# Reordering the prologue of a chunked recurrence: the first triangular inverse ahead of the last two preparations

## The chip, the cores and the metric

The kernel runs on one core of a Trainium2 chip. The metric is the device time of one execution in microseconds. The core has five engines that matter here, each with an instruction queue worked in order: TensorE (PE), VectorE (DVE), ScalarE (ACT), GpSimd (POOL), and SyncE (SP), which issues the DMA transfers. Instructions of different engines are ordered by semaphores alone.

## The reference, cut to what matters

A matrix-valued recurrence is followed by a small mixture of four attention experts. The recurrence has 4 batches of 8 heads, 768 steps and head size 40:

```python
for t in range(S):
    y[:, :, t] = einsum('bhd,bhde->bhe', r_t, state)
    Sa = einsum('bhde,bhe->bhd', state, a_t)
    state = state * w_t[:, :, None, :] - einsum('bhd,bhe->bhde', Sa, b_t)
    state = state + einsum('bhd,bhe->bhde', v_t, k_t)
```

Its output, with the heads side by side, is `x` (4 x 768 x 320). Each expert computes causal softmax attention over `x`; two of the four experts count for each token, weighted by a gate. The change touches the recurrence alone.

## The kernel before, in words

**Chunks, windows, units.** The 768 steps are cut into 24 chunks of 32 steps. Four chunks make a window (6 windows). The 32 (batch, head) pairs make 4 groups of 8. A unit is one chunk of one group: 96 units, unit u being chunk u // 4, group u % 4. A window therefore holds 16 units.

**Preparations.** For each window and group there is a preparation (`prep(i)`, i = 4 x window + group, 24 in all). Its pieces have one-letter names, and the schedule strings are made of them: `a` suffix scan of the decays (DVE, L249, into the tile SUF), `c` reciprocal (DVE), `s` prefix scan (DVE, L255), `x` scaled a (DVE, L259 or L263, into AB), `k`, `l` scaled k and b (DVE, L268, into KB) or `p`, both at once on POOL (L265), `b` a small copy (ACT), `d`, `q` copies of AB into the tile GL (ACT for i < 8, POOL L274 after), `m`, `n` products of KB and AB on TensorE (L284 or L286) whose results DVE masks into GL (L288, two multiplications each), `o` two DMAs of a part of GL to DRAM (L293, tensor Ld), `w`, `e`, `v` DMA loads of the inputs of preparation i + 1.

**Inverses.** Each window needs the inverse of unit triangular 32x32 matrices. `L` fetches them from Ld into the tile MT (L304, SP), `C` sets the diagonal (POOL memset, L306), `T5` issues five of the row instructions (L320), `A`, `D`, `E` (or `A`, `B`) transpose column ranges of MT into TT (DVE, L322). The first inverse does half of the rows on DVE (28 instructions) and the rest with products on TensorE (`P`, `F`, `H`). Inverses 1 to 5 run all 60 row instructions on POOL, where each depends on the one before. Window W needs inverse W from its first unit on (step `u` reads TT), and inverse W needs the four preparations of window W.

**The order.** All engines follow one order of issue. `START` is the prologue, read from left to right. Then the loop counts n from 0 to 99. For each n it issues seven steps, each of another unit, in the order of `MAIN`: `u` of unit n - 1, `g` of unit n, `y` of n - 3, `f` of n - 2, `t`, `k`, `v`. After each step it issues the jobs that were put into that slot with `at(n, slot, ...)`: slots 0 to 6 are the slash-separated fields of the strings in `EARLY`, `SIDE`, `SIDE2` and `INV`, so that `///6mno` stands in slot 3, behind the step `f`. `SIDE`, `SIDE2` and `INV` are relative to n0 = 16 (W - 1). Step `f` ends with a mask multiplication on DVE (L409), for which the step `y` of the next n waits.

**Loads.** Inputs of the preparations go to three tiles, EW, EA and EK. The first eight preparations borrow space of other tiles (`E8`) so that their loads need not wait; `own` are the tiles of all the later ones. A load into `own` waits for the preparation that read it before.

Of the kernel before, what the change touches and what calls it, by code (L numbers as in the profile page):

```python
# [17 lines left out]
NW, NG, C = 6, 4, 32  # L18
NKB = 10

START = """Z0 E4 0acsxklb E5 E7 E6 1acsxkl W2 0d 0q 1b 2ap 0mno 2csx W4 1d 1q 2b 3ap 1mno 3csx W0 2d 2q 4ap W1 3b 2mno 3mno L W3 V00 V10 3d 3q
4csx W5 W6 5ap C 4b 4mno V01 V11 5csx Z1 4d 4q Y0 6ap 5b 5mno k0 g0 6csx 5d 5q Y1 7ap E8 6b 6mno 7csx T14 7mno 7b 6d 6q Y2 T14 A B P F0 8ac H0 7d 7q Y3 8s 8w 8x 8v"""
EARLY = {
    1: "////F1",
    2: "////H1",
    4: "////F2",
    5: "////H2",
    7: "////F3",
    8: "////H3",
# [19 lines left out]
}  # L49

SIDE2 = {
    -16: "///0bkl///0e",
    -15: "///1ac",
    -14: "///1s///1w",
    -13: "///1x///1v",
    -12: "///1bkl///1e",
    -11: "///2ac 0m",
    -10: "///2s 1m///2w",
    -9: "///2bx///2v",
    -8: "///2kl///2e",  # L60
    -7: "///3ac 2m",
    -6: "///3s///3w",
    -5: "///3bx///3v",
    -4: "///3kl 0no//0dq/3e",
    -3: "///3m 1no//1dq",
    -2: "///2no//2dq",
    -1: "///3no//3dq",
}
INV = {0: "L C T5", 1: "T5", 2: "T5", 3: "T5", 4: "T5", 5: "T5", 6: "T5", 7: "T5", 8: "T5", 9: "T5", 10: "T5///A", 11: "T5", 14: "///D", 16: "E"}


def layouts(r, k, v, w, a, b):
# [47 lines left out]
def recurrence(tc, ctx, I, xT, CM, early, tail=None):  # L120
# [5 lines left out]
    V, A, T, PL = nc.vector, nc.scalar, nc.tensor, nc.gpsimd  # L126

    def ps(shape):
        return pp.tile(shape, F32, name="ps", tag="ps", bufs=4)
# [4 lines left out]
    def ring(name, shape, n):  # L134
        return [sp.tile(shape, F32, name=f"{name}{i}") for i in range(n)]
# [7 lines left out]
    D1P = ring("D1P", [104, 528], 1)[0]  # L143
    SUF = ring("SUF", [104, 529], 1)[0]
    PC2 = ring("PC", [104, 2, 4], 6)
    SC2 = ring("SC", [104, 2, 16, 33], 6)
    PC, SC = ([t[k // 2][:, k % 2] for k in range(12)] for t in (PC2, SC2))
    KB = ring("KB", [128, 16, 64], NKB)
# [9 lines left out]
    LS = ring("LS", [128, 32, 40], 2)  # L158
# [4 lines left out]
    XT = ring("XT", [104, 8, 128], 2)  # L163
# [3 lines left out]
    flat = lambda t: t.rearrange("p a b -> p (a b)")  # L167
# [3 lines left out]
    own = (EWr[0], EAr[0], EKr[0])  # L171
    thirds = lambda t: (t[:, 0:528], t[:, 528:1040], t[:, 1040:2064])
    E8 = [own, thirds(r20), (flat(SC[11]), flat(LS[1])[:, 0:512], g1[:, 0:1024]), thirds(r21),
          (flat(SC[8]), flat(XT[1][:, 4:8]), flat(KB[8])), (flat(SC[9]), flat(XT[1][:, 0:4]), flat(KB[9])), own, (flat(SC[10]), flat(LS[1])[:, 512:1024], flat(XT[0]))]

    SUFs = SUF, flat(TT[0])[0:104, 0:529]

    def load_e(i, k):
        if i < 24:
            t = (E8[i] if i < 8 else own)[k]  # L180
            src, c0 = (("EA", 0), ("EA", 528), ("EK", 0))[k]
            nc.sync.dma_start(t[0:104], I[src][i, :, c0:c0 + t.shape[1]])
# [56 lines left out]
    def prep(i):  # L239

        w, g = divmod(i, NG)
        ab, sc, kb, pc = ABr[i % 4], SC[i % 12], KB[i % NKB], PC[i % 12]
        gl = GL[w % 2]
        SUF = SUFs[1 if i in (1, 3, 5, 7) else 0]
        sv = SUF[:, 1:529].rearrange("p (n c) -> p n c", c=33)
        EW, EA, EK = (x[0:104] for x in (E8[i] if i < 8 else own))
        ea = EA.rearrange("p (n c) -> p n c", c=32)
        def f0a():
            V.tensor_tensor_scan(SUF[:, 0:528][:, ::-1], EW[:, ::-1], d1[:, ::-1], 1.0, op0=OP.mult, op1=OP.add)  # L249
        def f0b():  # L250
            A.activation(pc, sv[:, ::4, 0], AF.Copy)
        def f0c():
            V.reciprocal(D1P[:, 0:528:132], sv[:, ::4, 0])
        def f1():
            V.tensor_tensor_scan(sc.rearrange("p n c -> p (n c)"), EW, D1P, 0.0, op0=OP.mult, op1=OP.add)  # L255
        aa = flat(ab)[0:104, 0:512].rearrange("p (n c) -> p n c", c=32)
        def f2():
            if i < 8:
                V.tensor_tensor(aa, ea, sc[:, :, 0:32], op=OP.mult)  # L259
                return  # L260
            for s in range(2):
                q = slice(64 * s, 64 * s + 40)
                V.tensor_tensor(ab[q, :, 32 * s:32 * s + 32], ea[q], sc[q, :, 0:32], op=OP.mult)  # L263
        def fp():
            PL.tensor_tensor(kb[0:104].rearrange("p n (k c) -> p n k c", k=2), EK.rearrange("p (n k c) -> p n k c", n=16, k=2),  # L265
                             sv[:, :, None, 1:33].to_broadcast([104, 16, 2, 32]), op=OP.mult)
        def fk(k):
            V.tensor_tensor(kb[0:104, :, 32 * k:32 * k + 32], EK.rearrange("p (n k c) -> p n k c", n=16, k=2)[:, :, k], sv[:, :, 1:33], op=OP.mult)  # L268
        def f5(s):
            o, q = gl[64:104, g, :, s, :], slice(64 * s, 64 * s + 40)  # L270
            if i < 8:
                A.activation(o, aa[q], AF.Copy)
            else:
                PL.tensor_copy(o, ab[q, :, 32 * s:32 * s + 32])  # L274
        def mm(c):
            p_a = ps([128, 4, 2, 32])
            o = gl[0:64, g].rearrange("q (p c) s t -> q p c s t", p=4)
            for p in range(4):
                for x in range(2):
                    n = p * 4 + c + x  # L280
                    if i < 8:
                        for s in range(2):
                            q = slice(64 * s, 64 * s + 40)
                            T.matmul(p_a[64 * s:64 * s + 64, p, x], kb[q, n, :], aa[q, n, :], start=True, stop=True, tile_position=(64 * s, 64 * s))  # L284
                    else:
                        T.matmul(p_a[64 * x:64 * x + 64, p], kb[0:104, n, :], ab[0:104, n, :], start=True, stop=True, tile_position=(0, 64 * x))  # L286
            for x in range(2):
                V.tensor_tensor(o[:, :, c:c + 2, x] if i < 8 else o[:, :, c + x], p_a[64 * x:64 * x + 64],  # L288
                                maskn[x][:, None, None, :].to_broadcast([64, 4, 2, 32]), op=OP.mult)
        def f6():  # L290
            for s in range(2):
                b = 64 * (g // 2) + 32 * s + 16 * (g % 2)
                nc.sync.dma_start(Ld[w % 2][b:b + 16].rearrange("n j t -> j n t"), gl[32:64, g, :, s])  # L293
        def load(k):
            load_e(i + 1, k)
        return dict(a=f0a, b=f0b, c=f0c, s=f1, x=f2, p=fp, k=lambda: fk(0), l=lambda: fk(1), d=lambda: f5(0), q=lambda: f5(1),
                    m=lambda: mm(0), n=lambda: mm(2), o=f6, w=lambda: load(0), v=lambda: load(1), e=lambda: load(2))
# [156 lines left out]
    def at(n, s, *fs):  # L454
        jobs.setdefault((max(n, 0), s), []).extend(fs)

    P = [prep(i) for i in range(24)]

    def run(i, names):
# [3 lines left out]
    for W in range(1, NW):  # L463
        n0 = 16 * (W - 1)
        inv = invert(W)
        for r, line in (SIDE if W > 2 else SIDE2).items():
            if W == 1:
                break
            for k, part in enumerate(line.split("/")):
                for z in part.split():  # L470
                    at(n0 + r, k, *[P[4 * W + int(z[0])][x] for x in z[1:]])
        for r, line in INV.items():
            for k, part in enumerate(line.split("/")):
                for z in part.split():
                    at(n0 + r, k, lambda z=z, inv=inv: inv[z[0]](*[int(x) for x in [z[1:]] if x]))
# [3 lines left out]
    def seq(line):  # L479
        for z in line.split():  # L480
            if z[0] == "E":
                for k in (0, 2, 1):
                    load_e(int(z[1:]), k)
            elif z[0] == "Y":
                zero(flat(ABr[int(z[1])])[:, 0:512])
            elif z[0] == "W":
                rest(int(z[1]))
            elif z[0] == "Z":
                zgl(int(z[1]))
            elif z[0] == "V":  # L490
                for k in (0,) if z[2] == "0" else (2, 1):
                    load_c(int(z[1]), k)
            elif z[0] == "k":
                units[int(z[1])]["k"]()
            elif z[0] == "g":
                units[int(z[1])]["g"]()
            elif z[0] in inv:
                inv[z[0]](*[int(x) for x in [z[1:]] if x])
            else:
                run(int(z[0]), z[1:])  # L500
# [7 lines left out]
    units = [unit(u) for u in range(NU)]  # L508
    seq(START)
    for n, line in EARLY.items():  # L510
# [473 lines left out]
```

## Time and profile before

| | |
|---|---|
| median of 3 runs | 638.88 us (636.87 to 639.97) |
| profiled execution | 635.57 us, span 633.8 us |
| PE, DVE, ACT, POOL busy over the span | 88%, 77%, 75%, 54% |
| first step `u` of a unit (L393) | 67.88 us |
| last row instruction of the fifth inverse ends | 324.07 us |

Times within the profile count from the start of its span. The last column of the stretches read below is the rate of the DMA engines in GB/s, the one before it their busy share, and the one before that the granted TensorE clock as a share of full speed.

### The profile page before, as it was taken

Reading aid. Unit: us, or ns where it says so; the run is one execution under the profiler, and the core shown is the slowest. Engines: PE = TensorE matmul, PEld = TensorE weight load, DVE = VectorE, ACT = ScalarE, POOL = GpSimd, SP = SyncE. Lnnn points to the kernel's source line nnn. Section 1 sums busy time; section 2 is a strip of 40 time slices with the busy share of each in tenths; the row PEclk is TensorE's granted clock in tenths of the full one; section 3 lists DMA queues with packets and bytes.
Section 4 is the critical chain, followed back from the end, with each engine's and each line's share of the span. In section 5 each row is a group of like instructions: output and inputs, shape, how many; then the busy total and the mean of one; then the engine's idle time right before and its main releaser. Section 6 shows DMA issues by size and latency. Waiting matters only on the chain. (4 is left out here: it accounts for less than half of the span.)

```text
span 633.8 us, 22437 instructions
## 1 busy us (share of the span) xinstructions
PE 558.9 (88%) x8849; PEld 480.2 (76%) x8849; DVE 488.9 (77%) x1150; ACT 477.2 (75%) x1299; POOL 345.4 (54%) x491
## 2 busy tenths in 40 slices
PE   6463899998998898899998997899899999999995
PEld 6463787886887787788886777778778778887774
DVE  7978678899999989986666947688885886677661
ACT  7991579899889879988999984576666666676763
POOL 2330399569989988988830101354662545243631
PEclk9555589999999999999999999899999999999999
DMA  7882344685678477545249716222321132102001
GB/s 224 240 195 50 103 114 113 142 206 155 138 184 185 114 186 192 144 95 174 74 146 259 212 39 167 51 63 76 83 60 47 39 89 66 47 12 61 32 33 49
DMA packets 63690, 73.84 MB, mean 117 GB/s; under 512 B 30168, under 2 KB 48344, under 8 KB 63576
## 3 DMA queue, kind: packets, MB, share of 16 engines
q1 hardware_dynamic: 63432, 72.21, 43.4%
q8 instruction: 73, 1.20, 0.8%
q14 instruction: 41, 0.34, 0.2%
q10 hardware_dynamic: 144, 0.10, 0.1%
HBM read 54.99 MB, written 11.01 MB: 104 GB/s over the span
## 5 line engine op out<-in xcount | busy, mean ns | idle before, releaser
L833 POOL TENSOR_TENSOR P<-P,m 128x128 f32<-128x128 f32 (+2 forms) x96 | 87.7, 935 | 95.4 <-DVE m L829 46.3
L320 POOL TENSOR_TENSOR MT<-MT,TP 128x30 f32<-128x30 f32 (+9 forms) x150 | 97.1, 647 | 11.8
L320 POOL TENSOR_TENSOR TP<-MT 128x30 f32<-128x30 f32 (+9 forms) x150 | 95.0, 633 | 11.6
L416 PE MATMUL py<-R,LS 128*40 128x80 f32 x1536 | 86.2, 238 | 4.2 <-DVE R L409 1.6
L822 ACT ACTIVATE P<-sc,m 128x128 f32<-128x128 f32 (+2 forms) x96 | 60.8, 634 | 29.8 <-DVE m L821 23.5
L821 DVE TENSOR_REDUCE m<-sc 128x1 f32<-128x128 f32 (+2 forms) x96 | 59.4, 622 | 20.1 <-PE sc L814 18.8
L416 PEld LDWEIGHTS py<-R,LS 128*40 128x40 f32 x1536 | 64.1, 119 | 13.1 <-ACT LS L446 5.1
L409 DVE TENSOR_TENSOR R<-ps,CM 64x128 f32<-64x128 f32 x192 | 54.9, 286 | 23.4 <-PE ps L406 19.7
L811 PE MATMUL sc<-ks,qs 128*128 128x384 f32 (+4 forms) x256 | 62.5, 345 | 5.4 <-ACT P L822 5.1
L395 ACT ACTIVATE R<-ps 32x160 f32<-32x160 f32 x192 | 56.7, 295 | 4.8 <-PE ps L393 0.8
L387 ACT ACTIVATE GT<-ps 32x160 f32<-32x160 f32 x192 | 56.6, 295 | 3.4
L841 PE MATMUL pt<-CM,P 128*128 128x128 f32 x336 | 51.9, 276 | 2.1 <-ACT pt L847 1.7
L406 PE MATMUL ps<-RB,VU 128*64 128x64 f32 x768 | 46.5, 229 | 2.7 <-ACT VU L401 1.9
L811 PEld LDWEIGHTS sc<-ks,qs 128*128 128x128 f32 x256 | 40.6, 189 | 10.8 <-ACT P L822 9.6
L393 PE MATMUL ps<-GT,TT 128*33 128x80 f32 x768 | 46.8, 243 | 2.0 <-ACT GT L387 1.0
L446 ACT ACTIVATE LS<-pt 40x320 f32<-40x320 f32 x92 | 39.6, 431 | 11.7 <-PE pt L442 8.9
L377 ACT ACTIVATE LS<-pt 64x320 f32<-64x320 f32 x96 | 41.5, 433 | 8.8 <-PE pt L373 7.3
L733 PE MATMUL pt<-xh,wq 128*128 128x384 f32 x192 | 43.0, 359 | 3.5 <-POOL xh L712 1.5
L859 PE MATMUL ot<-pt,vv 128*64 128x256 f32 (+1 forms) x384 | 43.5, 359 | 0.0
L442 PE MATMUL pt<-CM,R 104*104 104x104 f32 x368 | 42.8, 260 | 0.0
L406 PEld LDWEIGHTS ps<-RB,VU 128*64 128x64 f32 x768 | 36.7, 140 | 8.0 <-ACT VU L401 6.8
L847 ACT ACTIVATE pt<-pt 128x512 f32<-128x512 f32 (+1 forms) x64 | 34.5, 543 | 10.0 <-PE pt L841 8.8
(160 smaller groups left out, 1334.1 us busy)
## 6 DMA issues: line engine op xcount, KB each, us to landing
RB<-in_RB SPq DMA_DIRECT2D x24, 320.0 KB
EK<-in_EK SPq DMA_DIRECT2D x18, 416.0 KB
ks<-ks SPq DMA_DIRECT2D x32, 192.0 KB
R<-in_VG SPq DMA_DIRECT2D x24, 208.0 KB
EW<-in_EA SPq DMA_DIRECT2D x18, 214.5 KB
R<-in_VT SPq DMA_DIRECT2D x48, 80.0 KB
R<-in_RT SPq DMA_DIRECT2D x24, 160.0 KB
xT<-XT SPq DMA_DIRECT2D x48, 80.0 KB
```

Of the source, the lines that this page charges most:

```text
L320: return [lambda: e.tensor_tensor(tmp, row, col, op=OP.mult), lambda: e.tensor_tensor(o, o, tmp, op=OP.add)]
L387: A.activation(gt[b:b + 32, s::2], p_g[64 * s:64 * s + 32], AF.Copy)
L393: T.matmul(p_u[64 * x:64 * x + 33, y], tt[:, o:o + 33], gt[:, 2 * p:2 * p + 2], start=True, stop=True, tile_position=(0, 64 * x))
L395: A.activation(hd(r2[32:64, 40 * h0:40 * h0 + 320], 80)[:, x::2], p_u[64 * x:64 * x + 32], AF.Copy, scale=-1.0)
L406: T.matmul(p_f[64 * x:64 * x + 64, y], vu[:, p, :], rb[:, 4 * g + p, :], start=True, stop=True, tile_position=(0, 64 * x))
L409: V.tensor_tensor(o[:, :, x], p_f[64 * x:64 * x + 64], mask[x][:, None, None, :].to_broadcast([64, 2, 2, 32]), op=OP.mult)
L416: T.matmul(py[64 * s:64 * s + 40, p], ls[:, h, :], m, start=True, stop=True, tile_position=(0, 64 * s))
L811: T.matmul(ps[:, c, 0:cw], QS[b][:, e, o], KS[b][:, e, z, k], start=(z == 0), stop=(z == 1 and not last), skip_group_check=True)
L821: V.tensor_reduce(m[:, 0, t:t + 1], ps[:, 0:ch, 0:cw], axis=AX.XY, op=OP.max, negate=True)
L822: later(DE, lambda: A.activation(pv, ps[:, 0:ch, 0:cw], AF.Exp, bias=m[:, 0, t:t + 1], accum_out=m[:, 1, t:t + 1]))
L833: PL.tensor_tensor(P[:, 0:n], P[:, 0:n], m[:, 3, t:t + 1].to_broadcast([128, n]), op=OP.mult)
L841: T.transpose(p[:, 128 * y:128 * y + 128], st["P"][t][:, 128 * c:128 * c + 128], ident)
```

## The change

Preparations 6 and 7 leave the prologue in good part. The rows of the first inverse (`T10`, `T18`) and its transposes (`A B P`) now stand directly behind `5csx` and `5mno`. Preparation 6 follows them: its `acsxpb` ends the prologue, its `mno` comes in loop step n = 0. Preparation 7 is spread over n = 0 to 3 and uses the `own` tiles and the first SUF tile. Its load `E7` is the last item of `START`; `E6` comes after `V10`. The second inverse (W = 1), which fetched at n = 0 and issued five rows a unit from there on, fetches at n = 4 and issues its 60 rows at once; its last transpose `E` moves from slot 0 to slot 3 of n = 16. Preparations 8 to 11 are moved from the end of the prologue and n = 0 to 15 to n = 3 to 16, with the last `n o` and all eight POOL copies at n = 16. The third inverse (W = 2) starts at n = 17, not 16.

```diff
-START = """Z0 E4 0acsxklb E5 E7 E6 1acsxkl W2 0d 0q 1b 2ap 0mno 2csx W4 1d 1q 2b 3ap 1mno 3csx W0 2d 2q 4ap W1 3b 2mno 3mno L W3 V00 V10 3d 3q
-4csx W5 W6 5ap C 4b 4mno V01 V11 5csx Z1 4d 4q Y0 6ap 5b 5mno k0 g0 6csx 5d 5q Y1 7ap E8 6b 6mno 7csx T14 7mno 7b 6d 6q Y2 T14 A B P F0 8ac H0 7d 7q Y3 8s 8w 8x 8v"""
+START = """Z0 E4 0acsxklb E5 1acsxkl W2 0d 0q 1b 2ap 0mno 2csx W4 1d 1q 2b 3ap 1mno 3csx W0 2mno 2d 2q 4ap W1 3b 3mno L W3 V00 V10 E6 3d 3q
+4csx 5a W5 4b W6 5p C 4mn V01 V11 5csx 5b Z1 T10 4o 5mno k0 g0 4d 4q Y0 5d 5q Y1 T18 A B P F0 H0 6acsx 6pb E7"""
 EARLY = {
-    1: "////F1",
-    2: "////H1",
-    4: "////F2",
+    0: "///6mno 7ac",
+    1: "///7sx 6d 6q Y2/F1",
+    2: "///7kl 7b E8/H1",
+    3: "///7mno",
+    4: "////F2 7d 7q Y3",
...
 SIDE2 = {
-    -16: "///0bkl///0e",
-    -15: "///1ac",
...
-    -3: "///3m 1no//1dq",
-    -2: "///2no//2dq",
-    -1: "///3no//3dq",
+    -13: "///0ac",
+    -12: "///0sx///0wv",
+    -11: "///0bkl///0e",
...
+    -2: "///3kl 1no///3e",
+    -1: "///2no 3m",
+    0: "///3no//0dq 1dq 2dq 3dq",
 }
 INV = {0: "L C T5", 1: "T5", ... 10: "T5///A", 11: "T5", 14: "///D", 16: "E"}
+INV1 = {4: "L C T60", 13: "///A", 15: "///D", 16: "///E"}
+INV2 = {1: "L C T5", 2: "T5", ... 11: "T5///A", 12: "T5", 14: "///D", 16: "E"}
...
-          (flat(SC[8]), ...), (flat(SC[9]), ...), own, (flat(SC[10]), flat(LS[1])[:, 512:1024], flat(XT[0]))]
+          (flat(SC[8]), ...), (flat(SC[9]), ...), own, own]
...
-        SUF = SUFs[1 if i in (1, 3, 5, 7) else 0]
+        SUF = SUFs[1 if i in (1, 3, 5) else 0]
...
-        for r, line in INV.items():
+        for r, line in (INV if W > 2 else INV1 if W == 1 else INV2).items():
```

## Rows read from the trace of the kernel before

**Rows 1.** Stretches: length; PE, PEld, DVE, ACT, POOL busy (count); clock, DMA share, GB/s.

```profile
72.82:115.98 43.16, 40.28 (x1055) 35.84 (x1056) 32.48 (x64) 34.45 (x107) 38.47 (x61) 0.86 0.40 106
184.23:230.46 46.23, 41.55 (x933) 36.32 (x933) 42.77 (x90) 41.30 (x125) 41.48 (x61) 1.00 0.69 161
289.30:324.10 34.80, 34.79 (x763) 30.89 (x762) 21.76 (x69) 32.04 (x94) 30.08 (x61) 1.00 0.38 109
```

**Rows 2.** Timeline of POOL around the second and third inverse: start, length, instruction.

```profile
72.82 0.15 POOL L306 MEMSET MT<- 128x32 f32 x1 [24.18 <-DMA MT<-Ld]
120.21 1.28 POOL L274 COPY GLe<-AB 40x512 f32<-40x512 f32 x2 [0.28 <-ACT LS L446]
130.95 0.16 POOL L306 MEMSET MT<- 128x32 f32 x1 [9.46 <-DMA MT<-Ld]
```

**Rows 3.** Timeline of DVE where windows 1 and 2 begin.

```profile
122.29 0.88 DVE L288 TENSOR_TENSOR GLe<-ps,CM 64x256 f32<-64x256 f32 x2
123.41 0.63 DVE L322 STREAM_TRANSPOSE TT<-MT 128x256 f32<-128x256 f32 x1
176.95 0.65 DVE L322 STREAM_TRANSPOSE TT<-MT 128x256 f32<-128x256 f32 x1 [0.57 <-POOL MT L320]
```

**Rows 4.** Timeline of DVE in the prologue.

```profile
37.59 0.69 DVE L259 TENSOR_TENSOR AB<-XT,SC 104x512 f32<-104x512 f32 x1
...
52.03 0.18 DVE L320 TENSOR_TENSOR TP<-MT 128x28 f32<-128x28 f32 x1
...
54.44 0.26 DVE L320 TENSOR_TENSOR MT<-MT,TP 128x100 f32<-128x100 f32 x1
...
55.96 1.86 DVE L288 TENSOR_TENSOR GL<-ps,CM 64x256 f32<-64x256 f32 x4
...
61.51 0.21 DVE L320 TENSOR_TENSOR MT<-MT,TP 128x28 f32<-128x28 f32 x1
...
63.72 0.99 DVE L324 STREAM_TRANSPOSE TT<-MT 128x512 f32<-128x512 f32 x1
```

**Rows 5.** Timeline of SP: issues of the first two inverses' transfers.

```profile
23.78 8.50 SPq L293 DMA_DIRECT2D Ld<-GLe  x8
33.76 0.35 SPq L304 DMA_DIRECT2D MT<-Ld  x1
...
69.23 0.35 SPq L304 DMA_DIRECT2D MT<-Ld  x1
```

**Rows 6.** Timeline of PE in the prologue.

```profile
10.26 2.06 PE L284 MATMUL ps<-AB,KB 40*64 40x32 f32 x64
...
38.43 3.63 PE L284 MATMUL ps<-AB,KB 40*64 40x32 f32 x64 [3.29 <-DVE AB L259]
...
64.86 1.05 PE L331 MATMUL ps<-TT,TT 16*32 16x16 f32 x64 [8.97 <-DVE TT L324]
...
67.88 0.75 PE L393 MATMUL ps<-GT,TT 128*33 128x80 f32 x8 [0.45 <-ACT TT L340]
```

**Rows 7.** Timeline of POOL: three instructions that bear on shared time with DVE.

```profile
46.45 2.19 POOL L265 TENSOR_TENSOR KB<-XT,TT 104x1024 f32<-104x1024 f32 x1 [3.65 <-DVE TT L249]
...
74.25 1.28 POOL L320 TENSOR_TENSOR TP<-MT 128x84 f32<-128x84 f32 x1
75.62 0.36 POOL L320 TENSOR_TENSOR MT<-MT,TP 128x84 f32<-128x84 f32 x1
```

**Rows 8.** Timeline of DVE in the first units.

```profile
73.52 0.61 DVE L409 TENSOR_TENSOR R<-ps,CM 64x128 f32<-64x128 f32 x2 [1.70 <-PE ps L406]
74.16 1.26 DVE L255 TENSOR_TENSOR_SCAN SC<-EW,D1P 104x528 f32<-104x528 f32 x1
...
78.51 0.61 DVE L409 TENSOR_TENSOR R<-ps,CM 64x128 f32<-64x128 f32 x2 [3.09 <-PE ps L406]
```

**Rows 9.** One stretch for PE alone: length, busy (count), clock, DMA share, GB/s.

```profile
81.00:82.00 1.00, 1.00 (x46) 0.96 0.05 10
```

More of the change, by code (lines that the diff above doesn't have):

```diff
@@ L51 @@
 SIDE2 = {
-    -16: "///0bkl///0e",
-    -15: "///1ac",
[L54 to L64, printed above, removed]
-    -3: "///3m 1no//1dq",
-    -2: "///2no//2dq",
-    -1: "///3no//3dq",
+    -13: "///0ac",
+    -12: "///0sx///0wv",
+    -11: "///0bkl///0e",
+    -10: "///1ac 0m",
+    -9: "///1sx///1wv",
+    -8: "///1bkl 2ac///1e",
+    -7: "///2s 1m///2w",
+    -6: "///2bx///2v",
+    -5: "///2kl 3ac///2e",
+    -4: "///3s 2m///3w",
+    -3: "///3bx 0no///3v",
+    -2: "///3kl 1no///3e",
+    -1: "///2no 3m",
+    0: "///3no//0dq 1dq 2dq 3dq",
 }
 INV = {0: "L C T5", 1: "T5", 2: "T5", 3: "T5", 4: "T5", 5: "T5", 6: "T5", 7: "T5", 8: "T5", 9: "T5", 10: "T5///A", 11: "T5", 14: "///D", 16: "E"}
+INV1 = {4: "L C T60", 13: "///A", 15: "///D", 16: "///E"}
+INV2 = {1: "L C T5", 2: "T5", 3: "T5", 4: "T5", 5: "T5", 6: "T5", 7: "T5", 8: "T5", 9: "T5", 10: "T5", 11: "T5///A", 12: "T5", 14: "///D", 16: "E"}
 def layouts(r, k, v, w, a, b):
@@ L173, in recurrence @@
     E8 = [own, thirds(r20), (flat(SC[11]), flat(LS[1])[:, 0:512], g1[:, 0:1024]), thirds(r21),
-          (flat(SC[8]), flat(XT[1][:, 4:8]), flat(KB[8])), (flat(SC[9]), flat(XT[1][:, 0:4]), flat(KB[9])), own, (flat(SC[10]), flat(LS[1])[:, 512:1024], flat(XT[0]))]
+          (flat(SC[8]), flat(XT[1][:, 4:8]), flat(KB[8])), (flat(SC[9]), flat(XT[1][:, 0:4]), flat(KB[9])), own, own]
     SUFs = SUF, flat(TT[0])[0:104, 0:529]
```

## Prediction

> **What bounds the kernel now.** I read the page's slices first. DVE and ACT are near full in the prologue, PE is thinly used until about 68 us, and POOL works almost without a break from about 72 to 324 us. That last point is what the whole-span share (54%) hides, so I went to POOL's timeline. In the recurrence POOL runs the inverses, 60 dependent row instructions each, and between them eight copies. The stretches show three kinds of inverse [rows 1]: the second (72.82 to 115.98) took 43.2 us, the fourth 46.2, the last 34.8, all with POOL busy but for issue gaps. They differ by the DVE work beside them: 32.5, 42.8 and 21.8 us of it.
>
> Next, who waits at the window borders. Unit 32 needs the third inverse. The transpose that delivers it waited 0.57 us for POOL's last row (the row at 176.95) [rows 3]; from there on POOL has no idle time up to the last inverse. So POOL's chain sets the pace of windows 2 to 4, with DVE just behind, and a start of the third inverse that comes later or earlier passes to the end of the recurrence nearly one for one. Earlier, POOL does have gaps: it stood idle until 72.82, and from the end of its copies at 121.49 until 130.95, each time for a fetch of MT [rows 2]. The prologue matters only as far as it moves the third inverse's start at 130.95. This start hangs on the last masking of preparation 11, which ended at 123.17, 7.8 us earlier [rows 2, 3].
>
> **The change part by part.** The sum runs along the profiled execution (span 633.8, time 635.57); its difference is then put on the median of 638.88, which lies 3.3 above that execution.
>
> *Prologue.* DVE is the engine in question, and nothing in front of the first inverse's rows is removed from it but 6a, 6csx, 7acsx and their masks. `5x` ends at 38.28. The first ten row instructions took 52.03 to 54.70, or 2.7: to 41.0. The masks of preparation 5 wait for its products, 38.43 + 3.63 = 42.06, and end about 43.0. The other 18 rows: 52.03 to 61.72 is 9.7, less the first ten and a break of 1.9, leaves 5.1: to 48.1. The three transposes took 61.72 to 64.71: to 51.1 [rows 4, 6]. That is 13.6 us earlier than 64.71. MT must be there at 38.3: it was fetched at 33.76, and a fetch takes 3.6 (69.23 to 72.82), so it is there at 37.4 [rows 2, 5]. The cover is under 1 us, but with the loads E6 and E7 out of the early queue the fetch can only come sooner. If it came later still, DVE would stand at the first row and the delay would be paid in full.
>
> *Unit 0.* It began 3.2 us after the transposes [rows 4, 6], so 54.3 would be possible. But `6mno` is issued at n = 0, ahead of unit 0 on PE's queue. It needs `6acsx`: two scans of 1.26, 0.69 for `x`, small change, 3.5 in all [rows 4, 8], so 54.6, and `6p` on POOL, 2.19 [rows 7], which starts behind `6a`. POOL and DVE disturb each other: the row instruction that met a scan took 1.28 against 0.36 for the next one of its size, 0.9 longer [rows 7, 8]. Price of the meeting of `6p` with `6s`: nothing, up to the whole 2.1 (one after the other). It is nearest to that meeting of a row with a scan, so I take the long side, 1.7: products start at 56.3. The Trainium skill (SBUF — State Buffer, "Who interferes with whom") says the two engines share a port pair by exclusive lock, and that a DVE instruction with two SBUF inputs blocks a GpSimd instruction that reads SBUF, whichever is second waiting whole. The trace's 0.9 fits it; by the rule the meeting costs the full 2.1, without it 0, and my sum would move by +0.4 or -1.7.
>
> The products then take 3.63 at half clock or 2.06 at full clock [rows 6]; PE had been idle before, as at 38.43, so 3.63: unit 0 starts at 60.0, 7.9 us earlier than 67.88.
>
> *Preparation 7, n = 1 to 3.* In the trace the masks of step `f` came 5.6 and 10.6 us after unit 0 [rows 6, 8], so at 65.6 and 70.6; ACT's block of two copies and a zeroing stood ahead of unit 0's outputs then (7d 7q Y3) and does again (6d 6q Y2), at no new cost. `7sx` hides in DVE's wait before the first mask (1.70 of idle was there), `7kl` (1.3) in that before the second (3.09) [rows 8]. Behind the second come 8a and 8c, 1.5, while PE runs `7m 7n` behind the same step `f`: 70.8 + 3.63 (2.06 at full clock). Last mask of preparation 7: about 75.3; 73.9 at full clock.
>
> *Second inverse.* Its two stores and its fetch are next on SP. From the masks to the first POOL instruction: two issues 0.85, then from the last store to the fetch 1.5 (32.28 to 33.76), then 3.6, in sum 6.0 [rows 2, 5]; the other bound is the 7.8 of the third inverse, in heavier DMA traffic. With little loading then, 6.0: start 81.3 against 72.82, so 8.5 us later. The rows are no shorter for being issued at once: POOL did not wait for their issue before either [rows 1]. Length: 34.8 with no preparations beside it, 43.2 with about 3.7 of them (8s to 11n), so 2.3 each; now 3.3 lie beside it, about 42.2. Bounds 34.8 and 46.2 [rows 1]. End: 123.5. The transpose `E` now waits for it in slot 3 of n = 16 and ends at 124.2, against 124.04 before [rows 3]. On DVE, work up to there is the same and so are the waits, within about 3 us: it gets there at about 124 by itself. The 13.6 us are gone by then.
>
> *Third inverse.* `11n` and its stores now stand behind `E` in DVE's queue; before, they were done at 123.17, ahead of it. So 124.2 + 0.9 = 125.1, and 7.8 to the first row: 132.9 against 130.95. With the light traffic's 6.0 it would be 131.1. I take 132.6, nearer to the row of the same place. The eight copies, moved to n = 16, take 5 to 6 us on POOL (they ended at 121.49) and hide under this fetch; they cost only what they exceed it by. The third inverse then sets the end 1.6 us later: it had 0.57 us to give in the other direction only.
>
> *The rest.* E7 into `own`, the other SUF, the closer `SIDE2`, the rows of W = 2 one unit later: nothing, as POOL's own queue covers the last, and the loads are issued a unit or more ahead of their scans. On SP the fetch at n = 4 waits some 2 us for its stores, and holds behind it the loads of chunk 2 (used from n = 8 on) and of preparation 9 (scanned at n = 6): both have two units, some 7 us. Without that cover a load costs about 3.6 us once, by the fetch's row [rows 2, 5].
>
> Sum: 638.88 + 1.6 = 640.5. Range from the unknown prices: no lock -1.7, full clock -1.4 to -3, light traffic -1.8, against +1.8 (7.8 for the second fetch too) and +3.9 (length 46.2 for 42.2); together about -4 to +6.
>
> **The rivals.**
>
> *PE is fed earlier and gets its clock back earlier: faster.* The granted clock was half until the stretch 81 to 82, where it was 0.96, that is near 2.4 GHz [rows 9], after dense work from about 65 on; now dense work begins 10 us or more sooner. If 2.4 GHz is there for `6mno` and n = 1 to 3, both product blocks save 1.6, and the 10.6 us to the second mask lose about 2: the second inverse starts 5.2 sooner, at 76.1, and ends at 118.3. DVE then decides, since fewer PE waits speed it as well, and the third inverse starts near 127.5: 3.3 to 5 us gained, about 634.7. Against it: `6mno` has PE idle ahead of it, like all such blocks after 20 us, which ran at half.
>
> *The second inverse runs at the pace of the fourth: slower.* 46.2 in place of 42.2 because preparations 9 to 11 are packed against it. For it: the third to fifth all show that length under DVE loads of 42 us, and DVE is to be as full here [rows 1]. It adds 4.0 at `E`, hence at the third inverse: +5.6, 644.5. It decides from a length of about 44.
>
> *The change reaches nothing.* E and the third fetch fall where they were, because DVE, not POOL, leads up to n = 16 and the fetch is quicker: 638.9.
>
> **How the numbers follow.** A measurement here tells about 0.5%, 3.2 us, from no change. My forecast 0.40 (of it 0.06 end beyond +3.2), nothing reached 0.16, clock 0.18, longer inverse 0.20, other mishaps on the load queue, slower, 0.06. Forecast without its tail (0.34) and nothing reached give within 0.5%: 0.50; faster 0.18; slower 0.06 + 0.20 + 0.06 = 0.32. The range 635.0 to 645.0 takes in most of the two outer cases. For the forecast alone it would be 637.5 to 643.
>
> **What would show it.** Transposes of the first inverse end near 51; unit 0 near 60 (54 to 55 if `6mno` does not hold it); the second inverse's memset near 81 with a length of 41 to 44; `E` waiting for POOL at about 123.5; the third inverse's memset at 131 to 133; no POOL gaps after that. A memset of the second inverse before 77, or `E` not waiting, would make it wrong on the fast side; a third one after 135 on the slow side.

## The result and the profile after

Medians: 642.29 us after (639.89 to 645.86, 15 runs), 638.88 before (635.74 to 640.56, 15 runs). The medians lie 3.4 us apart; the ratio, of the means (642.67 to 638.36), is 1.0068, 95% interval [1.0044, 1.0091]: 0.7% slower, inside the predicted range, but about twice the forecast of +1.6 us and beyond the 0.5% that it stayed under. The profiled execution of the changed kernel took 644.33 us, 8.76 more than that of before; 5.4 of these come from which executions were profiled (3.3 below its median there, 2.0 above it here), which is why the traces below are compared place by place, against a second trace of the kernel before, and against one of the changed kernel with only the issue of the second inverse's rows altered.

The changed kernel's lines carry numbers two higher. First the timeline of DVE in its prologue: start, length, instruction, and in brackets the idle time before it with what ended it.

```profile
50.51 0.99 DVE L326 STREAM_TRANSPOSE TT<-MT 128x512 f32<-128x512 f32 x1
51.36 1.20 DVE L251 TENSOR_TENSOR_SCAN SUF<-EW,D 104x528 f32<-104x528 f32 x1
52.59 0.18 DVE L255 RECIPROCAL D1P<-SUF 104x4 f32<-104x4 f32 x1
52.81 3.12 DVE L257 TENSOR_TENSOR_SCAN SC<-EW,D1P 104x528 f32<-104x528 f32 x1
...
58.76 0.88 DVE L290 TENSOR_TENSOR GL<-ps,CM 64x256 f32<-64x256 f32 x2 [2.10 <-PE ps L286]
60.47 0.88 DVE L290 TENSOR_TENSOR GL<-ps,CM 64x256 f32<-64x256 f32 x2 [0.83 <-PE ps L286]
```

Beside it, PE: the products of preparation 6, unit 0, and the products of preparation 7.

```profile
56.80 3.63 PE L286 MATMUL ps<-AB,KB 40*64 40x32 f32 x64 [2.57 <-DVE AB L261]
60.36 0.75 PE L395 MATMUL ps<-GT,TT 128*33 128x80 f32 x8
...
70.86 2.44 PE L286 MATMUL ps<-AB,KB 40*64 40x32 f32 x64
```

The first inverse's transposes end at 51.50 in place of 64.71, and unit 0 starts at 60.36 in place of 67.88 [rows 4, 6]. What the move cost shows between them. The scan of preparation 6 took 3.12 us where the same scan takes 1.26 [rows 8], since POOL began `6p` (52.64 to 54.81) just before; and DVE then stood 2.10 and 0.83 us for the products of preparation 6. The kernel before stood 0.93 and 0.83 us for these products, with the scan `7a` in front:

```profile
45.12 1.25 DVE L249 TENSOR_TENSOR_SCAN TT<-SC,D 104x528 f32<-104x528 f32 x1
47.30 0.88 DVE L288 TENSOR_TENSOR GL<-ps,CM 64x256 f32<-64x256 f32 x2 [0.93 <-PE ps L284]
49.01 0.88 DVE L288 TENSOR_TENSOR GL<-ps,CM 64x256 f32<-64x256 f32 x2 [0.83 <-PE ps L284]
```

For the products of preparation 7 it did not stand at all: the rows of the first inverse lay there, up to the masks at 55.96 [rows 4].

Then POOL from the second inverse on, in the changed kernel:

```profile
81.56 0.15 POOL L308 MEMSET MT<- 128x32 f32 x1 [26.75 <-DMA MT<-Ld]
...
126.70 7.00 POOL L276 COPY GLe<-AB 40x512 f32<-40x512 f32 x8
136.93 0.16 POOL L308 MEMSET MT<- 128x32 f32 x1 [3.23 <-DMA MT<-Ld]
...
242.45 0.16 POOL L308 MEMSET MT<- 128x32 f32 x1 [0.77 <-DMA MT<-Ld]
...
295.98 0.16 POOL L308 MEMSET MT<- 128x32 f32 x1 [1.71 <-DMA MT<-Ld]
```

and DVE where window 1 begins (against [rows 3]):

```profile
121.56 0.59 DVE L411 TENSOR_TENSOR R<-ps,CM 64x128 f32<-64x128 f32 x2
122.18 0.65 DVE L324 STREAM_TRANSPOSE TT<-MT 128x256 f32<-128x256 f32 x1
122.86 1.78 DVE L290 TENSOR_TENSOR GLe<-ps,CM 64x256 f32<-64x256 f32 x4
...
125.67 0.59 DVE L411 TENSOR_TENSOR R<-ps,CM 64x128 f32<-64x128 f32 x2
126.67 0.63 DVE L324 STREAM_TRANSPOSE TT<-MT 128x256 f32<-128x256 f32 x1 [0.41 <-POOL MT L322]
127.33 0.88 DVE L290 TENSOR_TENSOR GLe<-ps,CM 64x256 f32<-64x256 f32 x2
```

The second inverse starts 8.7 us later (81.56 for 72.82), its `E` runs at 126.67 for 123.41, the last mask of preparation 11 at 127.33 for 122.29, and the third inverse starts 6.0 us later (136.93 for 130.95) [rows 2, 3]. From there the delay runs through: the last inverse (W = 5; in the table of the kernel before it is the fifth, counted from 0) starts at 295.98, 6.7 us later than the 289.30 of before [rows 1].

**Where the lead went.** The masks of step `f` show it. The first stood at 66.70 for 73.52, a lead of 6.8 us [rows 8]; the second led by 7.5, the third by 4.5 (77.47, after the products and masks of preparation 7), the eighth by 2.9, the twelfth by 1.6, the fourteenth by 0.1, and the fifteenth, at 125.67, came 0.9 after that of before (124.77). Up to this fifteenth mask, in the changed kernel and in the one before (one line each: length; PE, PEld, DVE, ACT, POOL busy with counts; clock, DMA share, GB/s):

```profile
0.00:125.67 125.67, 91.88 (x2140) 84.12 (x2140) 101.43 (x198) 94.57 (x208) 54.13 (x78) 0.73 0.58 146
```

```profile
0.00:124.77 124.77, 89.46 (x2138) 82.22 (x2139) 99.61 (x198) 94.00 (x207) 60.03 (x89) 0.73 0.56 148
```

DVE's idle time is 25.2 us before and 24.2 after, and its work is 1.8 us more: 1.29 for `7kl`, which was `7p` on POOL before, and 1.86 for the scan at 52.81, less 1.5 for two pieces that now stand behind this mask (`E` and `11n`), make 1.6 of it. The work repeats from trace to trace, the idle time does not. In the second trace of the kernel before, DVE worked 99.62 us up to its fifteenth mask at 122.87 and was idle for 23.3; in that of the changed kernel with the rows spread it worked 101.46 us up to 123.32 and was idle for 21.9. So nothing is left at this mask of the 13 us brought forward, the added 1.8 us of work is certain, and whether the mask itself comes later single traces do not tell.

### The profile page after: what moved, and what is told of

Same layout as the page of the kernel before. It is cut to its first block, busy times and chain, and to the rows that moved or that the text cites. A ratio compares the mean times of both kernels' runs of the same rounds, so it can differ in the third digit from the quotient of the medians.

```text
span 642.5 us, 22421 instructions
## 1 busy us (share of the span) xinstructions
PE 563.7 (88%) x8849; PEld 484.8 (75%) x8849; DVE 493.6 (77%) x1152; ACT 478.7 (75%) x1299; POOL 345.4 (54%) x490
## 5 line engine op out<-in xcount | busy, mean ns | idle before, releaser
L322 POOL TENSOR_TENSOR MT<-MT,TP 128x30 f32<-128x30 f32 (+9 forms) x150 | 101.8, 679 | 11.8
L322 POOL TENSOR_TENSOR TP<-MT 128x30 f32<-128x30 f32 (+9 forms) x150 | 91.8, 612 | 11.6
```

What stands on the lines that cost most here:

```text
L322: return [lambda: e.tensor_tensor(tmp, row, col, op=OP.mult), lambda: e.tensor_tensor(o, o, tmp, op=OP.add)]
```

## The experiments

Every ratio is against runs of the kernel before on the same chip.

**The masks of preparation 11 back in front of `E`** (changed kernel, preparation 11 and third inverse as before):

```diff
-    -1: "///2no 3m",
-    0: "///3no//0dq 1dq 2dq 3dq",
+    -1: "///2no 3mno",
+    0: "/////0dq 1dq 2dq 3dq",
...
-        for r, line in (INV if W > 2 else INV1 if W == 1 else INV2).items():
+        for r, line in (INV1 if W == 1 else INV).items():
```

> The changed kernel, with the last masks of preparation 11 back at n = 15, ahead of the transpose E, and the third inverse back at n = 16. Theory (the loss is the late start of the third inverse, most of it because preparation 11's masks stand behind E): third memset about 133.8 instead of 136.9, bound then by the eight copies that end near 133.7, and the time 3 us below the changed kernel, about 639. Rival (the loss is made in the first units, where preparations 6 and 7 now stand; the third inverse only follows): third memset at 136 to 137 and the time unchanged, about 642.

Measured: 1.011 [1.005, 1.017], no faster than the changed kernel. The third inverse's memset came 5.3 us earlier (131.66), but the eight copies were now queued behind its first rows and ran between the fifth and the sixth of them:

```profile
131.66 0.16 POOL L308 MEMSET MT<- 128x32 f32 x1 [4.65 <-DMA MT<-Ld]
...
133.96 0.33 POOL L322 TENSOR_TENSOR TP<-MT 128x84 f32<-128x84 f32 x1
134.35 7.89 POOL L276 COPY GLe<-AB 40x512 f32<-40x512 f32 x8
142.32 1.18 POOL L322 TENSOR_TENSOR MT<-MT,TP 128x84 f32<-128x84 f32 x1
```

So the edit took the gain away itself, and was made again with the copies ahead (the line of `INV` as above):

```diff
-    -1: "///2no 3m",
-    0: "///3no//0dq 1dq 2dq 3dq",
+    -1: "///2no 3mno//0dq 1dq 2dq 3dq",
```

> As the first experiment, but with the eight POOL copies issued at n = 15, ahead of the third inverse in POOL's queue: there they had landed between its fifth and sixth row and cost the inverse 8 us. Theory: the copies end at 133 to 134 under the fetch, the third memset comes at about 134 (changed kernel 136.9), and the time is some 3 us under the changed kernel, 0.2 to 0.3% over the kernel before. Rival (the first units are the cause): as the changed kernel, 0.7% over the kernel before.

Measured: 1.0052 [1.0025, 1.0079]. The third memset came at 134.08, 2.9 earlier than in the changed kernel, as forecast, now held by the copies, which cannot start before the second inverse's rows end (126.96). The time cannot be told from the changed kernel's 0.7%, nor, at the lower end of its interval, from the 0.3% that was expected. In its trace the gain did not last to the last inverse. POOL there:

```profile
287.11 5.29 POOL L275 COPY GL<-AB 40x512 f32<-40x512 f32 x8
296.30 0.15 POOL L307 MEMSET MT<- 128x32 f32 x1 [3.91 <-DMA MT<-Ld]
```

POOL was ready at 292.4 and waited 3.91 us for the fetch, that is for DVE's masks and the transfers behind them.

**Only the late preparation 11**, put into the kernel before (`3no` to n = 16, third inverse from n = 17):

```diff
-    -1: "///3no//3dq",
+    -1: "/////3dq",
+    0: "///3no",
```

> The kernel before, with one part of the change alone: preparation 11's last masks at n = 16 behind E, third inverse at n = 17. Theory: third memset 2 to 3 us later than 130.95 (124.0 + 0.9 + 7.8 to 8.7 is 132.7 to 133.6), time 2 to 3 us above the kernel before, about 641. Rival: no change, about 639.

Measured: 1.0022 [0.9992, 1.0052]. The profile shows the third memset at 135.36, 4.4 us later, with the fifteenth mask at 125.43; in time it cannot be told from no change, nor from +0.5%.

**The first inverse's rows moved, with all else still in the prologue**, in the kernel before: `START` with `T10` and `T18 A B P` ahead of preparations 6 and 7. The edit moves more than the rows: `6ap` loses its place ahead of `5mno`, and `7ap` its place ahead of `6mno`, so that nothing but the short `c` stands between `a` and `s` of either preparation any more.

```diff
-... 5csx Z1 4d 4q Y0 6ap 5b 5mno k0 g0 6csx 5d 5q Y1 7ap E8 6b 6mno 7csx T14 7mno 7b 6d 6q Y2 T14 A B P F0 8ac ...
+... 5csx 5b Z1 T10 5mno k0 g0 4d 4q Y0 5d 5q Y1 T18 A B P F0 H0 6apcsx 6b 6mno 7apcsx E8 7b 7mno 6d 6q Y2 8ac ...
```

> The kernel before with one part of the change alone: the first inverse's rows and transposes ahead of preparations 6 and 7, all of them still in the prologue, everything behind it as before. Theory (VectorE's work up to n = 16 is what counts, and its order does not shorten it): the transposes end near 51 but unit 0 still starts at 64 to 68, the third memset stays at 129 to 132 and the time within 0.3% of the kernel before. Rival (the earlier inverse helps and the later parts of the change take it back): 1% faster.

Measured: 1.0056 [1.0031, 1.0081], most of the whole loss, against the expectation. DVE in this kernel's prologue:

```profile
52.32 3.11 DVE L255 TENSOR_TENSOR_SCAN SC<-EW,D1P 104x528 f32<-104x528 f32 x1
55.46 0.69 DVE L259 TENSOR_TENSOR AB<-EA,SC 104x512 f32<-104x512 f32 x1
58.26 0.88 DVE L288 TENSOR_TENSOR GL<-ps,CM 64x256 f32<-64x256 f32 x2 [2.10 <-PE ps L284]
59.97 0.88 DVE L288 TENSOR_TENSOR GL<-ps,CM 64x256 f32<-64x256 f32 x2 [0.83 <-PE ps L284]
...
62.38 3.12 DVE L255 TENSOR_TENSOR_SCAN SC<-SC,D1P 104x528 f32<-104x528 f32 x1
...
68.33 0.88 DVE L288 TENSOR_TENSOR GL<-ps,CM 64x256 f32<-64x256 f32 x2 [2.10 <-PE ps L284]
```

Both scans now met a POOL multiplication (1.9 us each), and both blocks of products were waited out (2.10 and 0.83 each time, where the kernel before has 0.93 and 0.83 for preparation 6 and nothing for 7). Only the wait for the products of 7 had been filled by rows. What had kept the scans clear was the order of the preparations: the masks of the one before stood between `a` and `s`, as at 47.30 and 49.01 between `7a` and `7s`. A version with the rows ahead and `7ap` left in front of `6mno` was not run, so this 0.56% is that of the whole edit, not of the rows alone. Unit 0 started at 69.93, later than the 67.88 of before [rows 6], and the second inverse at 79.22. DVE had been busy for 103.35 us at its fifteenth mask (125.40), 3.7 more than before. The profiled execution (638.66 us) lies 3.4 below the median of this kernel.

**Second inverse in steps** (changed kernel, `T5` at each n from 4 to 15 in place of `T60` at n = 4):

> The changed kernel, with the second inverse's rows issued five per loop step again (n = 4 to 15), not 60 at once. Theory: no change (within 1 us of 642), second inverse 45 us long as before, since POOL never waited for their issue. Rival (60 rows in a block keep POOL from other work or make the inverse longer): length nearer 42 and up to 3 us faster.

Measured: 1.0057 [1.0029, 1.0084], not to be told from the changed kernel; start 80.76, end 125.53. Issuing 60 rows at once costs nothing that shows, as predicted. The engines' work is that of the changed kernel, so this is a second look at it, and it differs. The fifteenth mask and `E`:

```profile
123.32 0.59 DVE L411 TENSOR_TENSOR R<-ps,CM 64x128 f32<-64x128 f32 x2
125.57 0.63 DVE L324 STREAM_TRANSPOSE TT<-MT 128x256 f32<-128x256 f32 x1 [1.66 <-POOL MT L322]
```

DVE came to `E` at 123.91 and waited 1.66 us for POOL; in the trace of the changed kernel above it came at 126.26 and waited 0.41. The third memset lies at 134.21, 2.7 us earlier than there.

**Second inverse's fetch early**, in the kernel before: SP issues it right behind the stores of preparation 7 and no longer at n = 0.

```diff
-... T14 7mno 7b 6d 6q Y2 ...
+... T14 7mno J 7b 6d 6q Y2 ...
```

(`J` is the fetch `L` of that inverse.)

> The kernel before, with the second inverse's fetch issued right behind preparation 7's stores (it stood behind the loads of preparation 9, which wait for DVE). Theory: second memset near 64 instead of 72.8 and its end 9 us earlier, but the third memset stays at 130 to 131, since preparation 11's masks set it; time unchanged, about 639 (at most 1 us faster). Rival (the start of the second inverse sets the pace): time 5 to 9 us lower, about 631.

Measured: 1.0005 [0.9972, 1.0039]. POOL:

```profile
63.72 0.16 POOL L306 MEMSET MT<- 128x32 f32 x1 [14.90 <-DMA MT<-Ld]
...
127.57 0.15 POOL L306 MEMSET MT<- 128x32 f32 x1 [8.91 <-DMA MT<-Ld]
...
288.61 0.15 POOL L306 MEMSET MT<- 128x32 f32 x1 [2.50 <-DMA MT<-Ld]
```

The second inverse started 9.1 us earlier, the third 3.4, the last 0.7 (before: 72.82, 130.95, 289.30 [rows 1, 2]), with 2.50 us of waiting for the last fetch that the kernel before did not have. Against the second trace of the kernel before (73.60, 128.31, 286.74) it is 9.9 and 0.7 earlier and 1.9 later. Either way, what POOL had gained at the second inverse was not there at the last.

**Shorter second inverse, lighter DVE, and both** (changed kernel). The first leaves four of the second inverse's row steps out; the second puts `6kl` on DVE and `7p` on POOL:

```diff
-        t = [f for j in range(1, 31 if w else 15) for f in step(j)]
+        t = [f for j in range(1, 31 if w else 15) if w != 1 or not 13 < j < 18 for f in step(j)]
```

```diff
-... H0 6acsx 6pb E7"""
+... H0 6acsxkl 6b E7"""
...
-    0: "///6mno 7ac",
+    0: "///6mno 7acp",
...
-    2: "///7kl 7b E8/H1",
+    2: "///7b E8/H1",
```

> The changed kernel, with four of the thirty row steps (eight instructions, about 7 us) of the second inverse left out, so that this part of the computation is not done. Theory A (DVE reaches the transpose E late by itself; in the changed kernel E waited only 0.41 us for POOL): POOL ends its rows near 120, E still starts near 126.3, the third inverse's memset stays at 136 to 137, and the time stays at 1.005 to 1.009 of before. Theory B (the second inverse's 45.1 us in place of the forecast 42.2 is what costs): E starts near 124, the third memset comes at 134 or sooner, and the ratio falls to 1.004 or less.

> The changed kernel, with k and l of preparation 6 on DVE in place of p on POOL (its scan s then meets no POOL multiplication, 1.26 in place of 3.12) and preparation 7's k and l as p on POOL behind c: 1.86 + 1.29 us less on DVE, 1.29 more. Theory A: the second memset at 79.5 to 81, DVE would reach E about 1.9 us sooner, near 124.4, but POOL's rows end at 125 to 126, so that E comes 0.4 to 1.5 sooner; third memset 135.5 to 136.5, ratio 1.004 to 1.008. Theory B (locks and DVE's extra work cost nothing): memset 81.5, third memset 136.9, ratio 1.007.

> Both edits together: the second inverse without four of its row steps (left out of the computation) and the lighter DVE work. Theory A, two bounds close together: E near 124.4, third memset near 134.7, about 2 us sooner than in the changed kernel and more than either edit alone, ratio 1.003 to 1.006. If E stays near 126, what delays DVE is neither its work nor POOL, but the units.

Measured: shorter 1.0064 [1.0043, 1.0085]; lighter 1.008 [1.0055, 1.0106]; both 1.0047 [1.0028, 1.0066]. With the shorter inverse DVE found it ready and still came to `E` only at 125.18:

```profile
121.07 0.65 DVE L324 STREAM_TRANSPOSE TT<-MT 128x256 f32<-128x256 f32 x1
121.75 1.78 DVE L290 TENSOR_TENSOR GLe<-ps,CM 64x256 f32<-64x256 f32 x4
...
125.18 0.63 DVE L324 STREAM_TRANSPOSE TT<-MT 128x256 f32<-128x256 f32 x1
```

The inverse took 38.7 us in place of 45.1. Its third memset lay at 133.74, 3.2 us earlier than in the changed kernel (0.5 earlier than with the rows spread) and just inside what the theory of the long inverse had asked for, but its time is that of the changed kernel, and its last memset came at 296.73, after 3.61 us of waiting: shortening the inverse alone brings no time that the measurement shows. The lighter kernel did not test what it was meant to: its scan `6s` was back at 1.26, but `7s` met `7p` and took 3.13, so DVE had as much to do as ever. Of the two together the profile looks best (`E` at 124.06, third memset 132.73), though the profiled execution was the fastest of its eight, 3.0 us below their median; the time lies lowest among the changed versions, and the interval overlaps that of the changed kernel: a hint, not a proof.

**Two versions meant to beat both kernels.** Rows ahead of preparations 6 and 7, both of these with `p` in the prologue, `6mno` and `7mno` at n = 0 and 2, second fetch early, preparations 8 to 11 so packed that their masks come before `E`; the second version has `6mno` behind unit 0's step at n = 1.

> A version from what was learned: the first inverse moved forward as in the change, but preparation 7 up to its products follows 6 at once in the prologue, with its loads in borrowed tiles and its k and b scaled on POOL; its masks and the second inverse's fetch come at n = 2, preparations 8 to 11 end at n = 15 and the third inverse is back at n = 16. VectorE's waits in n = 0 to 3 (9 us in the changed kernel) are partly filled. Theory: second memset near 73, third memset 125 to 128, time 3 to 5 us under the kernel before (0.5 to 0.8%). Rival (waits only move): third memset at 131, time as before.

> The same, with the products of preparation 6 issued at n = 1, so that unit 0 does not stand behind them on TensorE. Unit 0 starts near 55 instead of 60. Theory: VectorE and the third fetch decide, so the time is within 1 us of the one before. Rival (the units' start decides): up to 4 us faster than that one.

Measured: 1.0136 [1.0103, 1.0169] and 1.0103 [1.0068, 1.0139], the slowest of all. The second inverse did start earlier than in the changed kernel (77.91 and 74.85), but DVE came to `E` at 134.71 and 133.36, and the third memset stood at 142.63 and 140.57. Most of this is waiting: up to its fifteenth mask DVE worked 103.14 and 104.35 us, 1.7 and 2.9 more than in the changed kernel, and was idle for 33.0 and 30.4 us in place of 24.2. Between 60 and 125 us it stood 18.5 and 17.5 us for the products of step `f`, where the changed kernel has 10.5. Why PE was late there was not tried.

**The kernel before once more**, unchanged:

> The kernel before, unchanged, as a control: ratio 1.000, its interval within 0.3% of it. A second trace of it shows how far the memsets of the five inverses move between executions: if the third lies more than 2 us from 130.95, or the fetch before the last takes 5 us and more where it took 3.7, single traces tell no differences of that size.

Measured: 1.0002 [0.9983, 1.002]; the profiled execution took 634.01 us, with the second memset 0.8 later than in the first trace (73.60) and the third 2.6 earlier (128.31). Its line for the same stretch, up to its fifteenth mask at 122.87:

```profile
0.00:122.87 122.87, 87.17 (x2139) 80.28 (x2140) 99.62 (x199) 93.89 (x207) 60.47 (x89) 0.74 0.60 150
```

DVE's work is the same to 0.01 us; its idle time is 23.3 in place of 25.2. Differences of 2 to 3 us at the third memset between single traces therefore say little. The two traces of the kernel before (130.95 and 128.31) and the two of the changed work (136.93 and, with the rows spread, 134.21) lie 3.3 to 8.6 apart, so a later third inverse is shown; the 2.9 of the repaired preparation 11 is not.

**All traces side by side** (us):

| kernel | 15th mask | third memset | last memset | that execution |
|---|---|---|---|---|
| before | 124.77 | 130.95 | 289.30 | 635.57 |
| before again | 122.87 | 128.31 | 286.74 | 634.01 |
| early second fetch | 121.94 | 127.57 | 288.61 | 635.00 |
| rows moved, in the prologue | 125.40 | 130.80 | 291.17 | 638.66 |
| only 11 late | 125.43 | 135.36 | 293.32 | 641.01 |
| changed | 125.67 | 136.93 | 295.98 | 644.33 |
| changed, second's rows spread | 123.32 | 134.21 | 293.75 | 641.10 |
| changed, 11 back | 125.76 | 131.66 | 297.11 | 643.32 |
| changed, 11 and copies ahead | 123.78 | 134.08 | 296.30 | 643.49 |
| changed, second shorter | 124.56 | 133.74 | 296.73 | 642.57 |
| changed, DVE lighter | 125.11 | 136.38 | 295.98 | 644.13 |
| changed, both | 123.44 | 132.73 | 290.91 | 636.16 |
| waits filled | 136.10 | 142.63 | 303.10 | 648.83 |
| waits filled, unit 0 ahead | 134.74 | 140.57 | 303.95 | 651.78 |

The last column is the fourth plus 345.3 to 348.4 in every row: the start of the last inverse tells the end to within about 3 us. The third memset does not fix the last: from one to the other it takes 158.0 to 160.5 us in nine rows, POOL's own work and up to 2.9 us of waiting, and 161.0 to 163.0 in the three where only POOL had been made early (early second fetch, 11 and copies ahead, second shorter). Two rows stand apart: 165.45 where the copies lay inside the third inverse (11 back), and 163.4, with 5.4 us of waiting for fetches, in the last one, where POOL was not early at all.

## Why the prediction was nearly right, and where it failed

| step | forecast | trace |
|---|---|---|
| first inverse's transposes end | 51.1 | 51.50 |
| products of 6 start (lock counted 1.7) | 56.3 | 56.80 (lock 1.86) |
| unit 0 | 60.0 | 60.36 |
| last mask of preparation 7 | 75.3 | 74.96 |
| second memset | 81.3 | 81.56 |
| second inverse's rows end | 123.5 | 126.64 |
| `E` ends | 124.2 | 127.30 |
| `11n` ends | 125.1 | 128.21 |
| third memset | 132.6 | 136.93 |

**Right: the prologue and the way of the loss.** Up to 81 us each step in the table fell within 0.5 us, the last two by luck: the products of 7 took 2.44 us in place of 3.63, but `8a` and `8c` held DVE until 73.07 and all four masks then stood in line (75.3 forecast, 74.96 measured), and from there to the second memset it took 6.6 us in place of 6.0. The scan that met `6p` ended 1.12 us after POOL's multiplication (55.93 and 54.81). The Trainium skill (SBUF — State Buffer, "Who interferes with whom") lets the second of the two engines wait whole; that end, and the scans of 3.11 to 3.13 us against 1.26 in ten of the kernels run, agree with it. As forecast, `E` waited for POOL, the lead was gone by then, `11n` stood behind `E`, the third inverse started later, and the delay passed to the end. The size of the delay did not fit: the third memset, forecast at 131 to 133, came at 136.93 (134.21 with the rows spread), and the prediction itself had called one after 135 wrong on the slow side.

**Failed: "On DVE, work up to there is the same and so are the waits ... it gets there at about 124 by itself."** In the trace it got there at 126.26 (126.67 less the 0.41 of waiting). The new slot is not the reason. `E` moved from slot 0 to slot 3 of n = 16, behind the fifteenth mask, which in the kernel before ends at 125.38:

```profile
124.77 0.61 DVE L409 TENSOR_TENSOR R<-ps,CM 64x128 f32<-64x128 f32 x2
```

But there `E` and `11n` (1.5 us) still stand ahead of it; without them it would be at about 124, as the prediction has it. (With `11n` alone behind it, in the run with only preparation 11 late, the mask came 2.2 us after the one before it, not 3.1.) The work is what the sentence had wrong. `7kl` had been `7p` on POOL, and the scan's 1.86, which I had counted on the way to unit 0, also stays in DVE's total: 3.15 us that are not in the sentence, of which 0.9 was won back in idle time in this trace. With the rows spread, 3.3 was won back, and DVE came at 123.91 after all.

**Mis-sized: the second inverse's length.** 42.2 was taken, with 41 to 44 as the sign and 44 as the length from which the rival of the longer inverse decides. It took 45.1, and 44.8 to 46.0 in the four other runs with all its rows and the moved start; its rows ended at 125.5 to 127.0 in place of 123.5, and `E` waited for them in all five, 0.39 to 2.63 us. I had counted preparations beside it, 3.3 for 3.7, and so less DVE work; the trace has more, 39.05 us for 32.5 (length; PE, PEld, DVE, ACT, POOL busy with counts; clock, DMA share, GB/s):

```profile
81.56:126.64 45.08, 38.80 (x974) 33.86 (x970) 39.05 (x78) 35.94 (x110) 40.45 (x61) 0.96 0.59 139
```

A straight line between the second and the fourth inverse of [rows 1], by DVE work, gives 45.1 for 39.05. This is an estimate, with a DVE figure that only the trace after gave. So the rival "the second inverse runs at the pace of the fourth" was right in part. POOL and DVE both came to `E` later than forecast, which of them by more differs from trace to trace, and the run with the inverse shortened by 6.4 us shows that POOL alone does not decide: DVE came at 125.15 there.

**The hand-off** was taken as 7.5 (132.6 less 125.1) and took 8.7 (128.21 to 136.93). On SP a pair of output stores (130.32) and a load (131.12) stood between the last stores of Ld and the fetch, one load more than before, and the fetch itself took 5.4 us (131.56 to 136.93) against 4.0 before. With the rows spread it took 7.1, so 7.5 lies inside what single traces show.

**The range** is not the sum of its terms. Added up they give -4.9 to -6.5 and +5.7 around 640.5, that is 634 to 646, where 635 to 645 is stated; the result lies inside both.

**Not weighed: what the old order had been filling.** I costed the rows' move as pure gain for unit 0. Made in the kernel before, together with the closer order of preparations 6 and 7, it costs 0.56%. In the kernel before the rows were what DVE did while PE computed the products of 7, and the masks of the preparation ahead were what kept the scans away from POOL's multiplications. The late preparation 11 alone measured 0.2%, not separable from nothing. The two together would be 0.8%, against 0.7 measured; that they add up is consistent with the runs, not shown by them.

**Half right: "a start of the third inverse that comes later or earlier passes to the end of the recurrence nearly one for one."** Later, yes (6.0 became 6.7 at the last memset). Earlier, no: three kernels gave 2.7 to 3.9 us back against the kernel that each was made from (161.04 against 158.35, 162.22 and 162.99 against 159.05; repeats of these two lie within 0.5), and in their traces POOL waits for the last fetch, which stands behind DVE's masks. I read this as POOL and DVE bounding windows 1 to 4 together; one row of the table, the last, does not follow from it.

**The clock rival** happened for about 3 us. PE's lines of the changed kernel (length, busy with count, clock, DMA share, GB/s):

```profile
70.00:72.00 2.00, 2.00 (x42) 0.56 0.76 229
72.00:74.00 2.00, 2.00 (x56) 1.00 0.24 72
74.00:76.00 2.00, 1.26 (x31) 0.79 0.06 11
76.00:78.00 2.00, 2.00 (x72) 0.50 0.33 55
...
80.00:82.00 2.00, 2.00 (x52) 0.50 1.00 246
82.00:84.00 2.00, 1.04 (x67) 1.00 0.55 136
```

Full clock (2.4 GHz) came at about 72, 9 us earlier than in the kernel before [rows 9], in the middle of the products of 7 (70.86 to 73.30), which took 2.44 and not 3.63; after PE's less busy stretch at 74 to 76 it fell to half (1.2 GHz) until 82.

What stays open: how much of the 0.7% each of the parts costs, since 0.2 and 0.56 have intervals of 0.25 to 0.3 either way; whether the rows ahead would cost anything with `6ap` and `7ap` kept apart from their scans, which no run tries; and how the 0.56% of that run builds up, as its profiled execution, a quick one, lies 1.9 or 4.4 us behind the two of before at the last memset.

## What to carry to other kernels

Before bringing a block forward, ask what idle time of the leading engine it removes and what work it adds: here 13 us of lead in the prologue were used up 15 units later, because DVE got 1.8 us more work, and its idle time fell by no more than traces of one kernel differ. Look for what the block had been filling (the wait for the products of 7) and what the order around it had kept apart (a scan and POOL's multiplication). To size a chain that runs beside another engine, use that engine's work beside it (39 us), not the number of jobs. And where two engines are close behind each other, an early start for one of them can be given back at a later hand-over: look at the last stage, not at the first.

## What the runs showed of the hardware

A DVE scan that started while POOL multiplied ended 1.1 us after POOL in the traces looked at: it was 3.12 us long when it began 0.17 us behind (52.81 and 52.64), and 1.93 when 1.36 behind. The second is from the second trace of the kernel before (scan at 43.39, `6p` at 42.03), so the old order kept the scans clear of POOL only as long as `6p` was not late.

The two traces of the kernel before differ by 1.9 us at the fifteenth mask with DVE's work equal, and the clock of PE goes with it. In the first it fell back to half after two less busy stretches:

```profile
84.00:86.00 2.00, 1.37 (x78) 1.00 0.45 91
86.00:88.00 2.00, 1.57 (x46) 0.98 1.01 264
88.00:90.00 2.00, 2.00 (x43) 0.50 0.33 66
90.00:92.00 2.00, 2.00 (x25) 0.67 0.38 123
```

In the second, after 1.06 and 1.91 us of work in the same stretches, it stayed at 1.00 throughout. DVE's waits for step `f` were 10.7 us in the one and 8.8 in the other. That the clock is the cause was not tried.

The fetch of MT, always of the same size, took from its issue to the waiting POOL instruction 3.24 us (issued at 60.48) and 5.82 us (at 282.79) in one and the same execution, that of the kernel with the early fetch. The 3.6 that I took for a price is one draw of these.
